# A GQA decode block over a long KV cache: the output weights of the last two heads loaded behind V and multiplied together

## The chip, the cores and the metric

The kernel runs on one core of one Trainium2 chip. The metric is the device time of one execution in microseconds (us). TensorE is written PE, VectorE DVE, ScalarE ACT, GpSimd POOL; SP is the sync engine, which here does nothing but issue loads and stores. All data is float32.

## The reference, cut to what matters

Two tokens (batch B = 2, one position each, width D = 512) pass through a decode block: layer norm, attention with 32 query heads over 8 cached key/value heads of 32768 positions, an output projection, and a gated side branch.

```python
xn = _layernorm(x)                                   # x [2, 1, 512]
q = (xn @ wq).reshape(B, 1, 32, 128)                 # wq [512, 4096]
k, v = k_cache, v_cache                              # [2, 8, 32768, 128], each head used by 4 query heads
p = softmax(einsum("bhqd,bhkd->bhqk", q, k) * 128 ** -0.5)
o = einsum("bhqk,bhkd->bhqd", p, v)
s = o.reshape(B, 1, 4096) @ wo                       # wo [4096, 512]
gate, up = xn @ W_gate, xn @ W_up                    # [512, 1792] each
g = silu((gate * (gate > 0) * up) @ W_down)          # [1792, 512]
return x + s * g
```

Nearly all bytes are the two caches: 2 x 8 x 32768 x 128 x 4 bytes, 268 MB each.

## The kernel before, in words

There are 16 groups, one for each pair of KV head `hk` and batch `b`; group `g` has `b = g % 2` and `hk = g // 2`, so the two batches of a head follow each other. Each group has eight tiles of K and eight of V, 4096 positions or 2 MB each: 128 tiles of each in all, tile `t` in group `t // 8`.

All large loads go through one queue, SP's (`load`, L123), into one ring of eight slots of 2 MB (`SLOTS`). A load is issued when its slot has been given up by whatever was in it eight loads earlier. The output weights of a head (`load_wo`, four query heads, 512 rows of wo, 1 MB) take a slot of the same ring.

The main loop runs over steps `s`. Step `s` transposes K tile `s` on DVE in two halves (`k_transposes`, L287, tile `kts`) and multiplies it with the queries on PE (`scores`, L298); DVE scales the scores into `sc` and keeps the running maximum (L308). The values of a tile come `OFF` = 9 steps later, since a group's softmax needs the maximum over its eight tiles: `maximum` (L314 and on), then `weights` for a tile (exponential on ACT, L338; a permuting matmul `pt` on PE, L342; a transpose `pts` on DVE, L346), then `values` (L355), which accumulates in `o_ps`. After a group's last V tile `sums` gives the reciprocal of the softmax sum, `take_o` (L377) scales `o_ps` into `os`, and `finish_group` brings the result into the layout of the projection: 16 small matmuls into `po` (L386) and two copies into `ot` (L396).

After the second batch of a head, `finish_group` also projects: 16 matmuls of `ot` with that head's weights into `py` (L401). For heads 0 to 6 DVE adds `py` to `yacc` (L410). For head 7 it forms the result: `res = py * gy` and `res += base` (L412, L413), where `gy` is the side branch and `base = yacc * gy + x` was made before (`make_base`, L423, L424). `res` holds the output in four quarters of 128 columns at partitions 0, 32, 64 and 96; four stores of 1 KB, one on POOL's queue, two on SP's and one on ACT's, write them out (L470).

The order of the loads is written out in the lists `ahead`: step `s` issues V tile `s - 6` and K tile `s + 3`, and the output weights of a head stand right behind the last V tile of its second batch. So the weights of head 6 stand in the middle of the stream, between a V tile and the next K tile, and those of head 7 behind everything. Behind the last K tile come eight whole V tiles and the last one, which is loaded in three pieces, of a half and two quarters (`LAST = (2, 1, 1)`); `values` multiplies these pieces one after the other. On each engine the instructions keep an order that is fixed when the program is built; it is close to the program's but not the same: small work such as head 6's projection is placed between the score matmuls of a later step.

Of the kernel before, what the change touches and what calls it, by code (L numbers as in the profile page):

```python
# [8 lines left out]
F32 = mybir.dt.float32  # L9
# [4 lines left out]
P = 128  # L14
# [3 lines left out]
NBLK = NC * NJ  # L18
TK = P * NBLK
LAG = 1  # L20
LAST = (2, 1, 1)
SLOTS = 8
DEPTH = 3
ALIGN = 512
# [3 lines left out]
def kernel(  # L28
# [12 lines left out]
    nc = tc.nc  # L41
    B, HKV, SK, DH = kc.shape
# [4 lines left out]
    NU = SK // TK  # L47
# [10 lines left out]
    const = ctx.enter_context(tc.tile_pool(name="const", bufs=1))  # L58
# [4 lines left out]
    ps_m = ctx.enter_context(tc.tile_pool(name="ps_m", bufs=2, space=PSUM))  # L63
# [19 lines left out]
    n = 1  # L83
# [24 lines left out]

    qt = const.tile([P, B, HKV, 4, Q], F32, name="qt")
    nc.vector.memset(qt, 0.0)  # L110
    ot = const.tile([P, 2, 2, 32], F32, name="ot")
    nc.vector.memset(ot, 0.0)
    yacc = const.tile([P, P], F32, name="yacc")
    nc.vector.memset(yacc, 0.0)
    gy = const.tile([P, P], F32, name="gy")
    base = const.tile([P, P], F32, name="base")
    res = const.tile([P, P], F32, name="res")
# [3 lines left out]
    KT, VT, ST, PT, KTS, NBIAS, LS, MX, WO = {}, {}, {}, {}, {}, {}, {}, {}, {}  # L121
    def load(dst, src):
        nc.sync.dma_start(dst, src)  # L123

    def group(g):
        return g % B, g // B

    def load_tile(dst, src, t, pieces):
        b, hk = group(t // NU)
        lo = (t % NU) * TK  # L130
        rows = src[b, hk, lo : lo + TK, :].rearrange("(p r) d -> p (r d)", p=P)
        flat = dst.rearrange("p c j d -> p (c j d)")
        c = 0
        for n in pieces:
            part = slice(c * NJ * DH, (c + n) * NJ * DH)
            load(flat[:, part], rows[:, part])
            c += n
# [5 lines left out]
    def load_v(t):  # L143
        VT[t] = ring.tile([P, NC, NJ, DH], F32, tag="r", align_bytes=ALIGN, name=f"v_{t}")
        load_tile(VT[t], vc, t, (NC,) if t < NG * NU - 1 else LAST)

    def load_wo(hk):
        WO[hk] = ring.tile([P, 2, 2, D], F32, tag="r", align_bytes=ALIGN, name=f"wo_{hk}")
        r = REP * DH
        load(  # L150
            WO[hk].rearrange("p c i d -> p c (i d)"),
            wo[hk * r : (hk + 1) * r, :].rearrange("(c p i) d -> p c (i d)", c=2, i=2),
        )


    QW = wq.shape[1] // 2
# [191 lines left out]
    def values(t):  # L348
        g, u = divmod(t, NU)
        v, w = VT.pop(t), PT.pop(t)  # L350
        c = 0
        for n in (NC,) if t < NK - 1 else LAST:
            for j in range(NJ):
# [24 lines left out]

    def finish_group(g):
        b, hk = group(g)  # L380
        pr = ps_m.tile([P, 512], F32, tag="m", name=f"po_{g}")
        o2 = OS.pop(g).rearrange("p c (q i) -> p c i q", i=2)
        for i in range(2):
            for r in range(2):
                for c in range(NC):
                    nc.tensor.matmul(  # L386
                        pr[64 * r : 64 * r + 64, i * REP : (i + 1) * REP],
                        o2[:, c, i, :],
                        sel[:, c, :],
                        start=(c == 0),  # L390
                        stop=(c == NC - 1),
                    )
        o3 = pr[:, : 2 * REP].rearrange("p (i c r) -> p c i r", i=2, r=2)
        for r in range(2):
            part = slice(64 * r, 64 * r + 64)
            nc.vector.tensor_copy(ot[part, :, :, b], o3[part, :, :, r])  # L396
        if b == B - 1:
            py = ps_m.tile([P, 512], F32, tag="m", name=f"py_{g}")
            for k in range(4):
                for c in range(4):  # L400
                    nc.tensor.matmul(  # L401
                        py[32 * c : 32 * c + 32, :P],
                        ot[:, k // 2, k % 2, :],
                        WO[hk][:, k // 2, k % 2, c * P : (c + 1) * P],
                        start=(k == 0),
                        stop=(k == 3),
                    )
            WO.pop(hk)
            if hk < HKV - 1:
                nc.vector.tensor_add(yacc, yacc, py[:, :P])  # L410
            else:
                nc.vector.tensor_mul(res, py[:, :P], gy)  # L412
                nc.vector.tensor_add(res, res, base)  # L413

    NK = NG * NU
    OFF = NU + LAG
    extra, ahead = {}, {}

    def at(where, s, f, *a):
        where.setdefault(s, []).append((f, a))  # L420
# [10 lines left out]
        at(ahead, i + 2 - DEPTH, load_gu, "u", i)  # L431
        at(ahead, i + 4 - DEPTH, load_d, i)
    for hk in range(HKV):
        at(ahead, (hk * B + B) * NU - 1 + OFF - DEPTH, load_wo, hk)
    at(extra, 2, mlp_gu, "g")
    at(extra, 4, mlp_gu, "u")
    at(extra, 4, mlp_h)
# [10 lines left out]
    for s in range(NK + OFF):  # L448
        v = s - OFF
        if s < NK:  # L450
            k_transposes(s)
            scores(s)
        if 0 <= v + 1 < NK:
            if (v + 1) % NU == 0:
                maximum((v + 1) // NU)
            weights(v + 1)
        for f, a in extra.get(s, []):
            f(*a)
        if v >= 0:
            if v % NU == NU - 1:  # L460
                sums(v // NU)
            values(v)
            if v % NU == NU - 1:
                take_o(v // NU)
                finish_group(v // NU)
        for f, a in ahead.get(s, []):
            f(*a)

    for c, eng in enumerate((nc.gpsimd, nc.sync, nc.scalar, nc.sync)):
        eng.dma_start(out[:, 0, c * P : (c + 1) * P], res[32 * c : 32 * c + B, :])  # L470


_INS = ["A_x", "A_k_cache", "A_v_cache", "A_wq", "A_wo", "B_W_gate", "B_W_up", "B_W_down"]
# [28 lines left out]
```

## Time and profile before

| | |
|---|---|
| time, median of 3 runs | 1333.25 us (1332.27 to 1333.82) |
| profiled execution | 1335.89 us |
| its span | 1334.0 us |
| granted PE clock, mean over the span | 0.841 |
| PE busy | 881.1 us (66%) |
| DVE busy | 736.5 us (55%) |
| ACT busy | 69.1 us (5%) |
| loads | 564.68 MB on SP's queue, 99.4% of the DMA engines' time |

The profile is of one execution. Its page gives the busy time of each engine, the clock granted to PE and the DMA rate over 40 equal slices of the span, and the costliest groups of instructions with the idle time ahead of them and what ended it. A timeline lists instructions in order of time: start, length, engine, line and operation, output and inputs, how many were merged, and in brackets the idle time before. A row of a stretch lists its start and end, its length, then for PE, PEld (weight loads), DVE, ACT and POOL the busy time with the number of instructions, then the granted clock (1.00 is full), the busy share of the DMA engines and GB/s. One matmul of float32 is two records on PE. A row of a single line gives the shortest, median and longest of its instructions in nanoseconds and when the first and last began; the row on landing gives the time from the issue of a load to its last byte.

### The profile page before, as it was taken

The numbers are of one execution on the slowest core, as the hardware profiler recorded it, in microseconds if no ns is written. First come the engines' busy times: TensorE is split into PE (matmuls) and PEld (weight loads), VectorE is DVE, ScalarE is ACT, GpSimd is POOL, SyncE is SP. The second block draws the span as 40 slices with busy tenths as digits, with TensorE's granted clock in tenths as the row PEclk, the third lists the DMA queues.
The fourth block names the chain that finished last, engine by engine and source line by source line (L and its number), as shares of the span: only waits on it lengthen the run. The fifth ranks groups of instructions, "written<-read, shape, count | busy, mean of one in ns | idle before, by whom it ended". The sixth has DMA issues, their size and how long they took to land.

```text
span 1334.0 us, 17338 instructions
## 1 busy us (share of the span) xinstructions
PE 881.1 (66%) x7560; PEld 345.6 (26%) x7560; DVE 736.5 (55%) x976; ACT 69.1 (5%) x261; POOL 1.3 (0%) x7
## 2 busy tenths in 40 slices
PE   4767566766757666676666757667666766767657
PEld 1333222222213222232222312223222232213213
DVE  5765554555555555564555555465565555556462
ACT  0001010100101001010100101001010100101001
POOL 0000000000000000000000000000000000000000
PEclk9777887988878888788977888888887978878889
DMA  9999999999999999999999999999999999999996
GB/s 397 429 431 429 431 430 430 429 431 431 429 430 431 430 430 430 429 430 432 430 430 422 428 430 431 429 416 429 429 430 430 415 430 429 431 431 414 430 430 283
DMA packets 40907, 565.79 MB, mean 424 GB/s; under 512 B 4462, under 2 KB 4478, under 8 KB 6784
## 3 DMA queue, kind: packets, MB, share of 16 engines
q1 hardware_dynamic: 40776, 564.68, 99.4%
q8 instruction: 60, 0.98, 0.3%
q14 instruction: 15, 0.12, 0.0%
q10 hardware_dynamic: 24, 0.01, 0.0%
q0 software_dynamic: 32, 0.00, 0.0%
HBM read 564.67 MB, written 0.00 MB: 423 GB/s over the span
## 4 chain that ended last, share of the span: by engine, by line
issue 100%; POOLq 0%; POOL 0%
POOLq L497 0%; POOL ident masks.py:199 0%; POOL ident masks.py:197 0%; POOLq masks.py:199 0%; POOLq L484 0%
## 5 line engine op out<-in xcount | busy, mean ns | idle before, releaser
L298 PE MATMUL s<-kts,qt 128*32 128x256 f32 x4096 | 466.7, 522 | 388.9 <-DVE kts L287 373.7
L287 DVE STREAM_TRANSPOSE kts<-k 128x2048 f32<-128x2048 f32 x256 | 572.7, 2275 | 0.0
L355 PE MATMUL o_ps<-v,pts 128*16 128x512 f32 (+2 forms) x2080 | 360.2, 675 | 0.0
L298 PEld LDWEIGHTS s<-kts,qt 128*32 128x32 f32 x4096 | 180.2, 140 | 664.3 <-issue 351.6
L308 DVE TENSOR_SCALAR_CACHE_REDUCE sc<-s 128x256 f32<-128x256 f32 x128 | 54.3, 425 | 375.5 <-PE s L298 375.5
L346 DVE STREAM_TRANSPOSE pts<-pt 128x256 f32<-128x256 f32 x128 | 57.0, 448 | 137.9 <-PE o_ps L355 131.2
L355 PEld LDWEIGHTS o_ps<-v,pts 128*16 128x16 f32 (+2 forms) x2080 | 96.2, 116 | 141.6 <-issue 130.1
L338 ACT ACTIVATE sc<-sc,nb 128x256 f32<-128x256 f32 x128 | 63.2, 494 | 1147.3 <-DVE nb L332 1147.3
L342 PE MATMUL pt<-sc,perm 128*128 128x256 f32 x256 | 85.3, 439 | 33.4 <-DVE pts L346 32.2
L342 PEld LDWEIGHTS pt<-sc,perm 128*128 128x128 f32 x256 | 42.5, 198 | 99.7 <-issue 73.0
L386 PE MATMUL po<-sel,os 128*64 128x4 f32 x512 | 23.4, 204 | 3.9 <-DVE os L377 3.9
L386 PEld LDWEIGHTS po<-sel,os 128*64 128x64 f32 x512 | 22.0, 138 | 10.2 <-DVE os L377 10.2
L338 ACT ACTIVATION_READ_ACCUMULATOR sc<-sc,nb 128x1 f32 x128 | 23.9, 187 | 0.0
L377 DVE TENSOR_SCALAR os<-o_ps,rl 128x512 f32<-128x512 f32 x16 | 12.0, 750 | 17.3 <-PE o_ps L355 17.3
L401 PE MATMUL py<-wo,ot 128*32 128x128 f32 x256 | 19.2, 403 | 0.4 <-DVE ot L396 0.4
L396 DVE COPY ot<-po 64x4 f32<-64x4 f32 x32 | 5.2, 163 | 19.7 <-PE po L386 19.5
L401 PEld LDWEIGHTS py<-wo,ot 128*32 128x32 f32 x256 | 14.1, 153 | 2.5 <-issue 1.5
L192 PE MATMUL pq<-wq,xnt 128*32 128x512 f32 x64 | 10.1, 788 | 1.1 <-DMA wq<-in_A_wq_dram 0.8
L308 DVE DVE_READ_ACCUMULATOR sc<-s 128x1 f32 x128 | 10.7, 83 | 0.0
L180 PE MATMUL px<-ident,boot 32*128 32x32 f32 x4 | 0.9, 288 | 12.8 <-DVE boot L174 12.8
L214 DVE COPY qt<-pqt 32x16 f32<-32x16 f32 x64 | 8.6, 176 | 1.3 <-PE pqt L209 0.9
L332 DVE COPY nb<-pr 128x1 f32<-128x1 f32 x16 | 2.5, 159 | 12.2 <-PE pr L328 12.2
(70 smaller groups left out, 115.3 us busy)
## 6 DMA issues: line engine op xcount, KB each, us to landing
k<-in_A_k_cache_dram SPq DMA_DIRECT2D x128, 2048.0 KB, 18.7
v<-in_A_v_cache_dram SPq DMA_DIRECT2D x127, 2048.0 KB, 17.2
wq<-in_A_wq_dram SPq DMA_DIRECT2D x4, 2048.0 KB, 13.3
wo<-in_A_wo_dram SPq DMA_DIRECT2D x8, 1024.0 KB, 15.5
wg<-in_B_W_gate_dram SPq DMA_DIRECT2D x2, 1792.0 KB
wu<-in_B_W_up_dram SPq DMA_DIRECT2D x2, 1792.0 KB, 33.0
wd<-in_B_W_down_dram SPq DMA_DIRECT2D x2, 1792.0 KB
v<-in_A_v_cache_dram SPq DMA_DIRECT2D x1, 1024.0 KB
```

The source lines that it names most:

```text
L192: nc.tensor.matmul(pq[half][32 * c : 32 * c + 32, :], xnt[:, k, :], wqt[k][:, half, c * 512 : (c + 1) * 512], start=(k == 0), stop=(k == N ...
L214: nc.vector.tensor_copy(qt[part, b, half * 4 : half * 4 + 4, :, kb * REP + h], src[:, :, :, b],)
L287: nc.vector.transpose(KTS[t][:, i * half : (i + 1) * half], src[:, i * half : (i + 1) * half])
L298: nc.tensor.matmul(ps[Q * c : Q * c + Q, :], qt[:, b, hk, e, :], mov[:, e, c], start=(e == 0), stop=(e == 3),)
L308: nc.vector.tensor_scalar(ST[t], ps, SCALE, None, op0=ALU.mult, op1=ALU.max, accum_out=MX[g][:, u : u + 1])
L338: nc.scalar.activation(st, st, AF.Exp, bias=NBIAS[g], scale=1.0, accum_out=LS[g][:, u : u + 1])
L342: nc.tensor.matmul(ps, perm.rearrange("p k c h -> p (k c h)"), st, start=True, stop=True)
L346: nc.vector.transpose(PT[t].rearrange("p j m -> p (j m)"), ps)
L355: nc.tensor.matmul(o_ps[a : a + n * REP, :n, :], w[:, j, c * REP : (c + n) * REP], v[:, c : c + n, j, :], start=(u == 0 and j < 4), stop=( ...
L377: nc.vector.tensor_scalar(OS[g], o_ps, RL.pop(g), None, op0=ALU.mult)
L386: nc.tensor.matmul(pr[64 * r : 64 * r + 64, i * REP : (i + 1) * REP], o2[:, c, i, :], sel[:, c, :], start=(c == 0), stop=(c == NC - 1),)
L401: nc.tensor.matmul(py[32 * c : 32 * c + 32, :P], ot[:, k // 2, k % 2, :], WO[hk][:, k // 2, k % 2, c * P : (c + 1) * P], start=(k == 0), s ...
```

## The change

Four things change.

- The output weights of head 6 are no longer loaded in the middle of the stream but, like head 7's, behind the last V tile; head 7's come after them, in two loads of half a megabyte.
- Head 6's projection is not made when its group ends. After the last group, one product over both heads, 32 matmuls accumulating in one `py`, is multiplied by `gy` and added to `base`. Only heads 0 to 5 go through `yacc`, so `base` can be made one head earlier. As the results of two heads must be kept, `ot` becomes `ots` with two places.
- The last V tile comes in two halves.
- Two stores of 2 KB, one for each batch row, on SP's and on ACT's queue, replace the four.

```diff
-LAST = (2, 1, 1)
+LAST = (2, 2)
...
-    ot = const.tile([P, 2, 2, 32], F32, name="ot")
-    nc.vector.memset(ot, 0.0)
+    ots = const.tile([P, 2, 2, 2, 32], F32, name="ots")
+    nc.vector.memset(ots, 0.0)
...
     def load_wo(hk):
...
-        load(
-            WO[hk].rearrange("p c i d -> p c (i d)"),
-            wo[hk * r : (hk + 1) * r, :].rearrange("(c p i) d -> p c (i d)", c=2, i=2),
-        )
+        dst = WO[hk].rearrange("p c i d -> p c (i d)")
+        rows = wo[hk * r : (hk + 1) * r, :].rearrange("(c p i) d -> p c (i d)", c=2, i=2)
+        if hk < HKV - 1:
+            load(dst, rows)
+        else:
+            for c in range(2):
+                load(dst[:, c], rows[:, c])
...
     def finish_group(g):
         b, hk = group(g)
+        ot = ots[:, hk % 2]
...
-        if b == B - 1:
-            py = ps_m.tile([P, 512], F32, tag="m", name=f"py_{g}")
+        if b == B - 1 and hk < HKV - 2:
+            py = project_o((hk,))
+            nc.vector.tensor_add(yacc, yacc, py[:, :P])
+        elif b == B - 1 and hk == HKV - 1:
+            py = project_o((hk - 1, hk))
+            nc.vector.tensor_mul(res, py[:, :P], gy)
+            nc.vector.tensor_add(res, res, base)
+
+    def project_o(hks):
+        py = ps_m.tile([P, 512], F32, tag="m", name=f"py_{hks[0]}")
+        for hk in hks:
+            w = WO.pop(hk)
             for k in range(4):
                 for c in range(4):
                     nc.tensor.matmul(
                         py[32 * c : 32 * c + 32, :P],
-                        ot[:, k // 2, k % 2, :],
-                        WO[hk][:, k // 2, k % 2, c * P : (c + 1) * P],
-                        start=(k == 0),
-                        stop=(k == 3),
+                        ots[:, hk % 2, k // 2, k % 2, :],
+                        w[:, k // 2, k % 2, c * P : (c + 1) * P],
+                        start=(hk == hks[0] and k == 0),
+                        stop=(hk == hks[-1] and k == 3),
                     )
-            WO.pop(hk)
-            if hk < HKV - 1:
-                nc.vector.tensor_add(yacc, yacc, py[:, :P])
-            else:
-                nc.vector.tensor_mul(res, py[:, :P], gy)
-                nc.vector.tensor_add(res, res, base)
+        return py
...
     for hk in range(HKV):
-        at(ahead, (hk * B + B) * NU - 1 + OFF - DEPTH, load_wo, hk)
+        end = hk if hk < HKV - 2 else HKV - 1
+        at(ahead, (end * B + B) * NU - 1 + OFF - DEPTH, load_wo, hk)
...
-    for c, eng in enumerate((nc.gpsimd, nc.sync, nc.scalar, nc.sync)):
-        eng.dma_start(out[:, 0, c * P : (c + 1) * P], res[32 * c : 32 * c + B, :])
+    rows = res.rearrange("(c q) n -> q c n", q=32)
+    for b, eng in enumerate((nc.sync, nc.scalar)):
+        eng.dma_start(out[b, 0, :].rearrange("(c n) -> c n", c=4), rows[b])
```

In the built program the 16 matmuls with head 6's weights stand on PE directly behind the last group's `po` matmuls and wait for their load alone; those with head 7's weights follow and wait for the two copies into `ots` and for their loads. On SP the first of the two loads of head 7's weights waits for the slot of the V tile eight loads ahead of it, the second tile of the last group.

## The prediction

> **What bounds the kernel now.** I read the page first, then the waits, the landings of single loads, and at last the timeline with the granted clock in short stretches. The chain that ended last is put down to "issue" for 100% of the span and tells nothing here.
>
> ```profile
> span 1334.0 us, 17338 instructions
> GB/s 397 429 431 429 431 430 430 429 431 431 429 430 431 430 430 430 429 430 432 430 430 422 428 430 431 429 416 429 429 430 430 415 430 429 431 431 414 430 430 283
> L287 DVE STREAM_TRANSPOSE kts<-k 128x2048 f32<-128x2048 f32 x256 | 572.7, 2275 | 0.0
> SPq L123 <- PE o_ps L355: 568.6, 120, 10.4
> ```
>
> The DMA engines move 430 GB/s nearly throughout, so the kernel looks bound by its loads. Yet the K transposes (L287), first reader of every K tile, never wait for one (idle 0.0); the load queue instead waits for the engines to free slots. So DVE and PE pace the loop, taking turns (the rows below show it), the loads keep up, and a load that comes earlier changes nothing by itself. The same holds near the end:
>
> ```profile
> L123 SPq DMA_DIRECT2D v<-in_A_v_cache_dram x7: 327/328/328, 1272.7 to 1298.2; - x7
> DMA to landing us min/median/max: 15.7/15.7/16.2
> 1311.38 1.91 PE L355 MATMUL o_ps<-v,pts 128*16 128x512 f32 x16
> L123 SPq DMA_DIRECT2D wo<-in_A_wo_dram x1: 378/378/378, 1310.2 to 1310.2; - x1
> DMA to landing us min/median/max: 15.5/15.5/15.5
> ...
> DMA to landing us min/median/max: 17.6/18.2/18.7
> ```
>
> The second of those seven V tiles, issued at 1278.0, lands at 1293.7 and is multiplied at 1311.38. The last wo, issued at 1310.2, lands at 1325.7. The last row is of the last V tile's small pieces, the longest there.
>
> What decides the pace is the granted clock. First the stretches in which a group *without* a projection works on its first K tile, then one *with* it (head 6's, the one that goes):
>
> ```profile
> 1149.72:1153.14 3.42, 2.09 (x20) 0.80 (x20) 1.74 (x2) 0.00 (x0) 0.00 (x0) 0.50 1.05 450
> 1153.14:1156.55 3.41, 3.41 (x26) 1.06 (x22) 0.43 (x2) 0.00 (x0) 0.00 (x0) 0.50 0.95 408
> 1156.55:1159.96 3.41, 1.72 (x12) 0.40 (x4) 2.31 (x2) 0.00 (x0) 0.00 (x0) 1.00 1.03 442
> ...
> 1224.82:1228.23 3.41, 3.01 (x39) 2.33 (x38) 1.91 (x7) 2.93 (x12) 0.00 (x0) 1.00 0.97 413
> 1228.23:1231.64 3.41, 2.59 (x16) 1.42 (x19) 3.41 (x3) 0.00 (x0) 0.00 (x0) 0.50 1.06 452
> 1231.64:1235.06 3.42, 3.42 (x51) 2.63 (x49) 1.93 (x5) 0.00 (x0) 0.00 (x0) 0.50 0.98 422
> 1235.06:1238.47 3.41, 2.76 (x31) 1.10 (x22) 1.35 (x4) 0.00 (x0) 0.00 (x0) 1.00 0.99 413
> 1241.88:1245.30 3.42, 2.85 (x28) 1.35 (x32) 0.51 (x1) 0.00 (x0) 0.00 (x0) 0.50 1.02 436
> 1245.30:1248.71 3.41, 2.76 (x22) 0.71 (x14) 1.62 (x4) 0.00 (x0) 0.00 (x0) 1.00 0.99 423
> ```
>
> The columns are the stretch, its length, busy PE, PEld, DVE, ACT, POOL, then the clock. Each stretch has one clock, 1.00 or 0.50. After a half-clock stretch in which PE was busy 2.09 or 2.59 us the next is again at 0.50; after 2.85, 3.41 or 3.42 us it is at 1.00.
>
> The Trainium skill ("TensorE: Matmul & The Clock Gate", Part 1) describes a free-running window of 3413 ns, a half clock after an idle window and a full one after a busy window; the rows agree, and show besides that "busy" means more than 2.59 of 3.41 us.
>
> **The change, part by part.**
>
> *Head 6's projection leaves the middle.* Sixteen matmuls and the addition to yacc go from the first step of the last group.
>
> ```profile
> 1140.29 0.16 DVE L314 TENSOR_REDUCE m<-mx 128x1 f32<-128x8 f32 x1
> 1155.15 0.42 DVE L308 TENSOR_SCALAR_CACHE_REDUCE sc<-s 128x256 f32<-128x256 f32 x1 [3.69 <-PE s L298]
> 1157.65 0.45 DVE L346 STREAM_TRANSPOSE pts<-pt 128x256 f32<-128x256 f32 x1 [2.07 <-PE o_ps L355]
> 1221.52 0.16 DVE L314 TENSOR_REDUCE m<-mx 128x1 f32<-128x8 f32 x1
> 1228.19 4.46 DVE L287 STREAM_TRANSPOSE kts<-k 128x2048 f32<-128x2048 f32 x2
> 1231.43 1.74 PE L401 MATMUL py<-wo,ot 128*32 128x128 f32 x26
> 1235.84 0.43 DVE L308 TENSOR_SCALAR_CACHE_REDUCE sc<-s 128x256 f32<-128x256 f32 x1 [1.45 <-PE s L298]
> 1237.56 0.45 DVE L346 STREAM_TRANSPOSE pts<-pt 128x256 f32<-128x256 f32 x1 [1.28 <-PE o_ps L355]
> 1293.37 0.42 DVE L308 TENSOR_SCALAR_CACHE_REDUCE sc<-s 128x256 f32<-128x256 f32 x1 [2.02 <-PE s L298]
> 1300.71 0.16 DVE L314 TENSOR_REDUCE m<-mx 128x1 f32<-128x8 f32 x1
> ```
>
> The projection sits at 1231.43, while PE would wait for the second half of the transposes (they end at 1232.65), so taking it out frees no time that counts. But it is what keeps PE busy for all of 1231.64 to 1235.06. Without it the scores alone fill that stretch from about 1232.7, 2.35 us, below the 2.59 us after which the clock stayed at half. So I expect 1235.06 to 1238.47 at 0.50 too. Then sc takes what it took in the group without a projection, 1155.15 less 1151.41 (transposes from 1146.95, as long), 3.74 us: 1232.65 + 3.74 = 1236.39. There pts came 2.50 us after sc, the half clock ending 1.40 us after sc; here it ends 2.08 us after, 0.68 us more, which costs 0.34 us: pts at 1239.23 instead of 1237.56, **+1.7 us**.
>
> What follows is paced by the same stretches. From one maximum (L314) to the next the group without projection takes 1221.52 - 1140.29 = 81.23 us, the one with it 1300.71 - 1221.52 = 79.19 us, a difference of 2.04 us. I take **+2.0 us** for the loop, near the +1.7 of its first step. The work then meets the stretches later than before, and one more can fall to half clock:
>
> ```profile
> 1304.44 1.46 PE L386 MATMUL po<-sel,os 128*64 128x4 f32 x32 [0.19 <-DVE os L377]
> 1308.20 1.91 PE L355 MATMUL o_ps<-v,pts 128*16 128x512 f32 x16
> ```
>
> Counted on in steps of 3.413 us from 1224.82, the stretches near the end have edges at 1306.74 and 1310.15. Two microseconds later, po runs from 1306.5 and the values product from 1310.2, so this stretch holds only po and the small transposing products, like 1224.82 to 1228.23, whose 3.01 busy microseconds were followed by 0.50. The values product then takes 3.5 instead of 1.91 us; a score product at half clock costs as much (sc waited 3.69 there, 2.02 at 1293.37). I take one such, **+1.6 us**; ends: none, 0, and two, +3.3.
>
> *The end.*
>
> ```profile
> 1324.60 1.63 PEld L355 LDWEIGHTS o_ps<-v,pts 128*8 128x8 f32 x44 [0.32 <-issue]
> 1327.40 1.46 PE L386 MATMUL po<-sel,os 128*64 128x4 f32 x32 [0.87 <-DVE os L377]
> 1328.89 0.34 DVE L396 COPY ot<-po 64x4 f32<-64x4 f32 x2 [1.55 <-PE po L386]
> 1329.29 0.81 PEld L401 LDWEIGHTS py<-wo,ot 128*32 128x32 f32 x32 [0.52 <-DVE ot L396]
> 1329.29 1.08 PE L401 MATMUL py<-wo,ot 128*32 128x128 f32 x32 [0.43 <-DVE ot L396]
> 1331.08 0.65 SPq L470 DMA_DIRECT2D out_dram<-res  x2
> 1331.35 0.65 POOL L470 DMA_DIRECT2D out_dram<-res  x1 [1330.04 <-DVE res L413]
> ```
>
> Head 6's product now stands behind po and ahead of head 7's. It needs nothing from the copies, so it starts when po ends (1328.86) and issues for 0.81 us; head 7's starts at 1329.67 instead of 1329.29: **+0.4 us**. Were it to wait for the copies, it would cost its whole 1.08. The last V tile in two pieces: 32 quarter-width records become 16 half-width ones. By columns the work is equal; the 44 small records went at 37 ns each, hardly above the matmuls' own pace. I take **-0.1** (ends -0.3 and 0). Stores: POOL's issue ends at 1332.00, SP's second at 1331.73, and a single SP issue, half of the pair's 0.65, at 1331.4. If a store lands equally long after its issue, 0.3 to 0.6 us go; four rows for a store instead of two could give 0.3 back. I take **-0.4** (ends -0.6 and 0).
>
> *What costs nothing.* Head 6's load leaves SP's queue ahead of the last group's K and V, which come earlier to engines that don't wait for them. At the end it stands behind V, and head 7's must wait for the slot of the V tile multiplied at 1311.38, free at 1313.3; at 15.5 us to landing this is 1328.8, ahead of 1329.67. That cover is only 0.9 us on the old timetable, some 4 us on mine. The doubled ots is cleared in the idle time before the first loads; the base computation moves one head earlier, beside a wait of sc for PE:
>
> ```profile
> 7.70 0.67 DVE L167 TENSOR_REDUCE st<-boot 32x1 f32<-32x512 f32 x1 [2.85 <-DMA boot<-in_A_x_dram]
> 1075.41 0.42 DVE L308 TENSOR_SCALAR_CACHE_REDUCE sc<-s 128x256 f32<-128x256 f32 x1 [2.11 <-PE s L298]
> ```
>
> **Sum.** +2.0 + 1.6 + 0.4 - 0.1 - 0.4 = +3.5 us: from the profiled execution's 1335.89 us (span 1334.0) to 1339.4. The plain runs have a median of 1333.25 (1332.27 to 1333.82), 2.64 lower; I put the same difference on it: 1336.7 us. No change that can be told is 0.2% here, 2.7 us.
>
> **The rivals.** *A, the forecast:* the clock stays at half one stretch longer. Chance 0.70, of which 0.20 for no further half stretch (+1.9 us, within 0.2%), 0.38 for one (+3.5) and 0.12 for two (+5.2).
>
> *B, the clock comes back as before.* If 2.35 us of unbroken score products are enough, the loop keeps its old times, and only the end counts: -0.1 us, 1333.1. Against it speak 2.09 and 2.59 us followed by 0.50; for it, that part of the 2.59 were transposing products, which may count less, as after 1224.82. It decides if the clock over 1235.06 to 1238.47 is 1.00. Chance 0.17. The Trainium skill's page on the clock gate, Part 1, read by its letter (only an idle window throttles) gives this case; here no row shows 2.35 us of scores alone.
>
> *C, faster:* without the projection the steps meet the stretches so that two fewer are at half clock. Each is worth at most 1.7 us (half of 3.41), so -0.1 - 3.4 = -3.5: 1329.8 us. For it speaks that steps with sc waiting 2.02 exist; against it, that less PE work makes the clock rise later and not sooner in every row above. Chance 0.10.
>
> *D, the last load is late:* if head 7's wo needs the 18.7 us of the slowest small piece from its slot at 1313.3 while the loop keeps its old pace, it lands at 1332.0, 2.3 us after its matmuls could start: 1333.1 + 2.3 = 1335.4 us. It decides from 16.4 us to landing on; 15.5 was measured. Chance 0.03.
>
> **How the numbers follow.** Slower by over 0.2%: 0.38 + 0.12 = 0.50. Within: 0.20 + 0.17 + 0.03 = 0.40. Faster: 0.10. The range goes from 1331.9 (B with the end's best terms, 0.4 - 0.3 - 0.6 = -0.5, and 0.8, half the spread of the runs) to 1338.9 (A with two half stretches, 1338.4, and half a microsecond towards the end's worst). It leaves out C and the extremes. A's own range is 1335.1 to 1338.9.
>
> **What would show it.** Right: no projection near 1231 us, the clock at 0.50 up to some 6 us past the end of that step's transposes, 81 us or more between the last two maxima. The final product in 64 records of some 1.9 us in all, its first half beside the copies, and no POOL store. Wrong: about 79.2 us between those maxima (B), fewer (C), or PE's last product waiting for a wo load (D).

## The result, and the profile after

The changed kernel takes 1336.59 us (median of 20 runs, 1330.48 to 1339.99), the kernel before, run beside it, 1333.67 us (20 runs, 1332.27 to 1336.53): a ratio of 1.0020, 95% interval 1.0013 to 1.0028, or 2.9 us more. The profiled execution took 1335.82 us with a span of 1334.0 us, the same span as before. This execution reached the steady part of its loop 3.35 us sooner than the one profiled before (1218.17 against 1221.52 us at the last maximum but one), and lost as much in the last group and the end. I take the head start for chance: the first maximum comes at 103.3 to 110.7 us in the thirteen profiles, and the medians differ by 2.9 us all the same. So intervals are compared here, and not points of time. One of the twenty runs, of 1330.48 us, had a mean granted clock of 0.852 where the others had 0.835 to 0.842; e2 comes back to it.

The timeline of the kernel after, DVE's part (start, length, engine, line and operation, names, and in brackets the idle time before it and what ended it); the maximum is line L317 here, the K transposes are L290, `sc` is L311 and `pts` L349:

```profile
1136.95 0.16 DVE L317 TENSOR_REDUCE m<-mx 128x1 f32<-128x8 f32 x1
1218.17 0.16 DVE L317 TENSOR_REDUCE m<-mx 128x1 f32<-128x8 f32 x1
1224.83 4.46 DVE L290 STREAM_TRANSPOSE kts<-k 128x2048 f32<-128x2048 f32 x2
1233.02 0.42 DVE L311 TENSOR_SCALAR_CACHE_REDUCE sc<-s 128x256 f32<-128x256 f32 x1 [3.69 <-PE s L301]
1235.88 0.45 DVE L349 STREAM_TRANSPOSE pts<-pt 128x256 f32<-128x256 f32 x1 [2.42 <-PE o_ps L358]
1300.30 0.16 DVE L317 TENSOR_REDUCE m<-mx 128x1 f32<-128x8 f32 x1
```

The interval ahead of the last one is 81.22 us, as before. The last one is 1300.30 - 1218.17 = 82.13 us, where it was 79.19. That is +2.94 us, as much as the medians differ by (2.92). The granted clock in the same place, in stretches of 3.41 us (columns as in the prediction: the stretch, its length, busy PE, PEld, DVE, ACT, POOL, then the clock):

```profile
1224.89:1228.30 3.41, 2.58 (x8) 0.84 (x6) 3.41 (x3) 0.00 (x0) 0.00 (x0) 0.50 1.00 428
1228.30:1231.72 3.42, 2.39 (x25) 1.15 (x28) 1.03 (x2) 0.00 (x0) 0.00 (x0) 0.50 1.02 436
1231.72:1235.13 3.41, 3.41 (x22) 0.82 (x16) 0.43 (x2) 0.00 (x0) 0.00 (x0) 0.50 0.99 418
1235.13:1238.54 3.41, 1.36 (x8) 0.30 (x2) 2.66 (x3) 0.00 (x0) 0.00 (x0) 1.00 1.04 447
1238.54:1241.96 3.42, 2.26 (x16) 0.81 (x20) 2.17 (x1) 0.00 (x0) 0.00 (x0) 0.50 0.97 417
1241.96:1245.37 3.41, 3.41 (x30) 1.26 (x26) 0.43 (x2) 0.00 (x0) 0.00 (x0) 0.50 1.01 432
```

The second of these is the stretch that held the projection and was busy for all of its 3.42 us. Now the scores alone keep PE busy for 2.39 us, the next stretch stays at 0.50, and the values product, which DVE's `pts` waits for, runs in it at half speed. The stretch after that holds only 1.36 us of work at full clock, and so the second step's scores, too, start at half clock; its first half-clock stretch is busy 2.26 us and again does not bring the clock back.

The end, from the timelines of before and of after:

```profile
1326.59 0.75 DVE L377 TENSOR_SCALAR os<-o_ps,rl 128x512 f32<-128x512 f32 x1 [4.72 <-PE o_ps L355]
...
1330.44 0.29 DVE L412 TENSOR_TENSOR res<-py,gy 128x128 f32<-128x128 f32 x1 [1.20 <-PE py L401]
1330.76 0.29 DVE L413 TENSOR_TENSOR res<-res,base 128x128 f32<-128x128 f32 x1
```

```profile
1326.17 0.75 DVE L380 TENSOR_SCALAR os<-o_ps,rl 128x512 f32<-128x512 f32 x1 [4.71 <-PE o_ps L358]
1328.37 1.95 PE L415 MATMUL py<-wo,ots 128*32 128x128 f32 x64
1328.48 0.34 DVE L400 COPY ots<-po 64x4 f32<-64x4 f32 x2 [1.55 <-PE po L390]
1330.39 0.29 DVE L406 TENSOR_TENSOR res<-py,gy 128x128 f32<-128x128 f32 x1 [1.57 <-PE py L415]
1330.72 0.29 DVE L407 TENSOR_TENSOR res<-res,base 128x128 f32<-128x128 f32 x1
1331.04 0.65 SPq L481 DMA_DIRECT2D out_dram<-res  x1
```

Counted from the last maximum, `os` comes after 1326.59 - 1300.71 = 25.88 us before and 25.87 after, so the last V tile in two halves changes nothing. `res` starts after 29.73 and 30.09 us: the longer product costs 0.36. From the end of the last DVE operation to the end of the span it is 1334.0 - 1331.05 = 2.95 and 1334.0 - 1331.01 = 2.99 us: two stores or four, it is the same.

### The profile page after: what moved, and what is told of

Same layout as the page of the kernel before. It is cut to its first block, busy times and chain, and to the rows that moved or that the text cites. A ratio compares the mean times of both kernels' runs of the same rounds, so it can differ in the third digit from the quotient of the medians.

```text
span 1334.0 us, 17305 instructions
## 1 busy us (share of the span) xinstructions
PE 880.8 (66%) x7544; PEld 341.9 (26%) x7544; DVE 736.4 (55%) x975; ACT 69.1 (5%) x261; POOL 0.7 (0%) x6
## 4 chain that ended last, share of the span: by engine, by line
PE 49%; DVE 46%; issue 3%; DMA 2%; ACT 0%; DVEq 0%
DVE kts L290 41%; PE s L301 25%; PE o_ps L358 18%; DVE pts L349 2%; PE po L390 2%; DMA wq<-in_A_wq_dram 2%; PE pt L345 1%; DVE sc L311 1%; PE py L415 1%; DVE os L380 1%; PE ps_g L239 0%; PE pr L331 0%; DVE qt L217 0%; PE pr L319 0%; PE pqt L212 0%
## 5 line engine op out<-in xcount | busy, mean ns | idle before, releaser
L290 DVE STREAM_TRANSPOSE kts<-k 128x2048 f32<-128x2048 f32 x256 | 572.8, 2275 | 0.0
L358 PE MATMUL o_ps<-v,pts 128*16 128x512 f32 (+1 forms) x2064 | 363.9, 686 | 0.0
L311 DVE TENSOR_SCALAR_CACHE_REDUCE sc<-s 128x256 f32<-128x256 f32 x128 | 54.3, 425 | 372.8 <-PE s L301 372.7
L349 DVE STREAM_TRANSPOSE pts<-pt 128x256 f32<-128x256 f32 x128 | 57.0, 448 | 140.8 <-PE o_ps L358 134.1
L358 PEld LDWEIGHTS o_ps<-v,pts 128*16 128x16 f32 (+1 forms) x2064 | 96.2, 117 | 144.6 <-issue 133.5
L415 PE MATMUL py<-wo,ots 128*32 128x128 f32 x256 | 17.5, 384 | 0.0
L400 DVE COPY ots<-po 64x4 f32<-64x4 f32 x32 | 5.2, 163 | 19.7 <-PE po L390 19.5
L415 PEld LDWEIGHTS py<-wo,ots 128*32 128x32 f32 x256 | 13.0, 146 | 1.8 <-issue 1.3
L311 DVE DVE_READ_ACCUMULATOR sc<-s 128x1 f32 x128 | 10.7, 83 | 0.0
L335 DVE COPY nb<-pr 128x1 f32<-128x1 f32 x16 | 2.5, 158 | 12.2 <-PE pr L331 12.2
## 6 DMA issues: line engine op xcount, KB each, us to landing
wq<-in_A_wq_dram SPq DMA_DIRECT2D x4, 2048.0 KB, 13.4
```

The costliest lines, as they stand in the source:

```text
L290: nc.vector.transpose(KTS[t][:, i * half : (i + 1) * half], src[:, i * half : (i + 1) * half])
L311: nc.vector.tensor_scalar(ST[t], ps, SCALE, None, op0=ALU.mult, op1=ALU.max, accum_out=MX[g][:, u : u + 1])
L349: nc.vector.transpose(PT[t].rearrange("p j m -> p (j m)"), ps)
L358: nc.tensor.matmul(o_ps[a : a + n * REP, :n, :], w[:, j, c * REP : (c + n) * REP], v[:, c : c + n, j, :], start=(u == 0 and j < 4), stop=( ...
L415: nc.tensor.matmul(py[32 * c : 32 * c + 32, :P], ots[:, hk % 2, k // 2, k % 2, :], w[:, k // 2, k % 2, c * P : (c + 1) * P], start=(hk == ...
```

## The experiments

Each is compared with runs of the kernel before made beside it on the same chip, whose medians were 1333.46 us (e1 to e4), 1332.90 (e5 to e8) and 1333.20 (e9 to e11). Theory A is the prediction's: the clock stays at half one stretch longer where the projection is missing.

**e1: head 6 back in the middle, the other edits kept.**

```diff
-        if b == B - 1 and hk < HKV - 2:
+        if b == B - 1 and hk < HKV - 1:
...
-            py = project_o((hk - 1, hk))
+            py = project_o((hk,))
...
-        end = hk if hk < HKV - 2 else HKV - 1
-        at(ahead, (end * B + B) * NU - 1 + OFF - DEPTH, load_wo, hk)
+        at(ahead, (hk * B + B) * NU - 1 + OFF - DEPTH, load_wo, hk)
```

> Undoes the move alone: head 6's weights are loaded and multiplied in the middle again, while the last V tile in two halves, the two loads of head 7's weights and the two stores stay as in the changed kernel. Theory A (head 6's product keeps PE busy in a stretch of 3.41 us, and so brings the clock back one stretch sooner): 79.2 us between the last two maxima, as in the kernel before; from the last maximum to the end 33.3 us; ratio to the kernel before 1.000, within 0.1%. Rival T (the end of the kernel pays: stores, pieces of V, weights behind V): the stores and the V pieces alone would show here as up to 1.002, with 79.2 us between the maxima and over 33.6 us behind the last one.

Measured: 1334.06 us, ratio 1.0005 (0.9997 to 1.0014). The last interval:

```profile
1220.34 0.16 DVE L317 TENSOR_REDUCE m<-mx 128x1 f32<-128x8 f32 x1
1299.52 0.16 DVE L317 TENSOR_REDUCE m<-mx 128x1 f32<-128x8 f32 x1
```

It is 79.18 us again. The V tile in halves, the two stores and the divided load of head 7's weights together move the time by nothing that can be told.

**e2: only the move.** The last V tile, head 7's load and the stores are those of before.

```diff
-LAST = (2, 2)
+LAST = (2, 1, 1)
...
-        if hk < HKV - 1:
-            load(dst, rows)
-        else:
-            for c in range(2):
-                load(dst[:, c], rows[:, c])
+        load(dst, rows)
...
-    for b, eng in enumerate((nc.sync, nc.scalar)):
-        eng.dma_start(out[b, 0, :].rearrange("(c n) -> c n", c=4), rows[b])
+    for c, eng in enumerate((nc.gpsimd, nc.sync, nc.scalar, nc.sync)):
+        eng.dma_start(out[:, 0, c * P : (c + 1) * P], res[32 * c : 32 * c + B, :])
```

> The move alone: both heads' weights behind V and multiplied together, but V in three pieces, head 7's weights in one load and four stores as in the kernel before. Theory A: about 82.1 us between the last two maxima, 33.7 us behind the last one, ratio to the kernel before 1.002. Rival T: if V's pieces, the split load or the stores are what costs, 1.000 to 1.001.

Measured: 1336.27 us, ratio 1.0012 (0.9997 to 1.0027). The interval includes no difference; it is wide because 4 of its 12 runs took 1331.0 to 1331.8 us and the others 1334.4 to 1339.8. In the profiled run, of 1335.35 us, the last interval is 82.12 us:

```profile
1217.75 0.16 DVE L313 TENSOR_REDUCE m<-mx 128x1 f32<-128x8 f32 x1
1299.87 0.16 DVE L313 TENSOR_REDUCE m<-mx 128x1 f32<-128x8 f32 x1
```

So in this execution the move alone makes the long interval. In the four shorter runs the mean granted clock was 0.849 to 0.856, in the others 0.838 to 0.842, so they met the clock otherwise, as did the one short run of after; no profile shows where.

**e3: the same work twice.** The kernel after, but head 6's weights are also loaded where they were before and multiplied there, and that product is thrown away.

```diff
+        elif b == B - 1 and hk == HKV - 2:
+            project_o((hk,))
...
+        if hk == HKV - 2:
+            at(ahead, (hk * B + B) * NU - 1 + OFF - DEPTH, load_wo, hk)
```

> The changed kernel, in which head 6's weights are loaded and multiplied in the middle as well, and that product is thrown away: 1 MB more to load, 16 matmuls more, no addition on DVE. Theory A: the useless product brings the clock back, so 79.2 us between the last two maxima, 33.7 us behind the last one, ratio to the kernel before 1.0003 (+0.4 us for the longer last product), some 2.5 us less than the changed kernel though it does more. Rival T: as the changed kernel or worse, ratio 1.002 to 1.004 (1 MB at 430 GB/s is 2.4 us). Rival D (the late loads of the weights hold up the last product): worse than the changed kernel by the 2.4 us that everything behind lands later.

Measured: 1334.78 us, ratio 1.0009 (1.0000 to 1.0017), and a last interval of 79.19 us:

```profile
1217.62 0.16 DVE L317 TENSOR_REDUCE m<-mx 128x1 f32<-128x8 f32 x1
1296.81 0.16 DVE L317 TENSOR_REDUCE m<-mx 128x1 f32<-128x8 f32 x1
```

With 1 MB more to load and 16 matmuls more, the last interval is 2.94 us shorter than after's. Work that nobody needs pays for itself. Only part of it reaches the end (1334.78 against 1336.59 us): the profile shows PE waiting 0.90 us for the last half of V, ahead of which 1 MB more was loaded, and `py` taking 2.96 us instead of 1.95.

**e4: no projection in the middle at all.** This kernel leaves out the projections of heads 0 to 6, matmuls and additions; their weights are still loaded.

```diff
-        if b == B - 1:
+        if b == B - 1 and hk == HKV - 1:
```

> The kernel before without the projections of heads 0 to 6, matmuls and additions (their weights are still loaded): it leaves out work that the output needs. Theory A: every group is then without a projection, seven of them take 81 to 82 us instead of 79.2, so +14 to +20 us, ratio 1.010 to 1.015. Rival W (PE or DVE work in the loop costs time, and less of it never hurts): ratio 1.000 or below, down to 0.990 (1.4 us for each product).

Measured: 1332.69 us, ratio 0.9995 (0.9987 to 1.0004). This expectation was far off. Without any projection the loop does not become slower by 2 to 3 us for each, but settles on another pattern:

```profile
1057.58 0.16 DVE L314 TENSOR_REDUCE m<-mx 128x1 f32<-128x8 f32 x1
1136.07 0.16 DVE L314 TENSOR_REDUCE m<-mx 128x1 f32<-128x8 f32 x1
1214.55 0.16 DVE L314 TENSOR_REDUCE m<-mx 128x1 f32<-128x8 f32 x1
1296.10 0.16 DVE L314 TENSOR_REDUCE m<-mx 128x1 f32<-128x8 f32 x1
```

Intervals of 78.49 and 78.48 us, with one of about 82 among them every few groups (three, besides one of 81.23 near the start and the last of 81.55). A group without a projection is therefore not long as such. The stretches of a short group, then of a long one:

```profile
1060.64:1064.05 3.41, 3.01 (x39) 2.17 (x38) 1.91 (x6) 3.17 (x14) 0.00 (x0) 1.00 0.97 413
1064.05:1067.47 3.42, 1.72 (x8) 0.73 (x8) 3.42 (x3) 0.00 (x0) 0.00 (x0) 1.00 1.04 441
1217.66:1221.07 3.41, 3.01 (x39) 2.17 (x38) 1.91 (x6) 3.12 (x14) 0.00 (x0) 1.00 0.95 408
1221.07:1224.48 3.41, 2.77 (x8) 1.24 (x8) 3.41 (x3) 0.00 (x0) 0.00 (x0) 0.50 1.06 447
1224.48:1227.90 3.42, 2.38 (x26) 1.02 (x28) 1.24 (x2) 0.00 (x0) 0.00 (x0) 0.50 1.01 431
```

The first stretch of each holds the same work, 3.01 us of it, but begins 3.06 us behind the maximum in the short group and 3.11 in the long one; after that the clock stays up in the one and falls in the other. This holds beyond e4. In the traces of all kernels but e5 and e6, that stretch is busy 3.01 or 3.02 us in 85 groups: in the 17 in which it begins 3.04 to 3.10 us behind the maximum the next is at full clock, in the 68 in which it begins 3.11 to 3.30 us behind it (3.30 in the last group of after) at half. (One of 2.98 us, in the second group of e7, fell at 3.08.) So the phase, the place of the stretches against the maximum, decides, and a group's time follows from it. What at the edge of the stretch makes the difference is open.

78.49 us are 23.0 stretches of 3.413 us and 82.0 are 24.0; in the kernel before two groups together, 160.42 us, are 47.0. The loop locks to the stretches of the clock, and an edit shifts it from one whole number to another.

**e5 and e6: PE kept busy in every step,** in the kernel before (e5) and in the kernel after (e6). In each K step two useless matmuls run between the first and the second half of the transposes.

```diff
         ps = ps_s.tile([P, 256], F32, tag="s", name=f"s_{t}")
+        pd = ps_m.tile([P, 512], F32, tag="m", name=f"pd_{t}")
+        for i in range(2):
+            nc.tensor.matmul(
+                pd[:, :384], ident, KTS[t][:, i * 512 : i * 512 + 384], start=(i == 0), stop=(i == 1)
+            )
```

> The kernel before, with two matmuls added in each of the 128 K steps that multiply the first half of the transposed tile (384 columns each) into a tile nobody reads, so that PE is busy while it waits for the second half of the transposes. Theory A (PE that is not busy enough in a 3.41 us stretch falls to half clock, and the half clocks pace the loop): the mean granted clock goes from 0.86 to above 0.95, the intervals between maxima (79.19 and 81.23 before) go to 79.0 or less, at the lowest what the loads allow (17 transfers of 2 MB in a group of 33.6 MB and half a wo at 430 GB/s, 79.2 us on average), and the run to about 1329 us (1326 to 1332), though PE does more work. Rival T (the work itself paces the loop, the clock only follows): two more matmuls of 0.5 to 1 us each in 128 steps make the run longer, 1340 us or more.

> The kernel after, with the same two matmuls in each K step. Theory A: the move costs what it does only by the half clock behind the removed projection. With the clock kept up there is no such stretch, the last interval between maxima is no longer than the others of this run, and this kernel stands within -2.5 to +0.5 us of the kernel before with the same additions (the last V tile lands some 2.4 us sooner, the end costs the 0.4 us measured). Rival (the move costs by itself, by its slot, its queue or its longer end): it is 2.5 to 3.5 us slower than the other one with additions, as after was against before.

Measured: e5 1332.03 us, ratio 0.9989 (0.9980 to 0.9999); e6 1331.43 us, ratio 0.9982 (0.9973 to 0.9991). More work in 128 steps makes both shorter, against rival T; but the mean clock rose only to 0.88, not above 0.95, and e5 stands at the upper bound of what was expected (1332). The list of waits of e5 says why:

```profile
DVE kts L287 <- DMA k<-in_A_k_cache_dram: 60.0, 37, 3.9
```

The K transposes now wait 60.0 us in all for their loads, 37 times; before they never did. The loads were only just hidden, and they take over as soon as the engines get faster. With the loads as the limit the move costs nothing: e6 is 0.6 us below e5, within the bounds expected of A. As the loads and not the clock pace both, this doesn't tell whether the clock is the cause; the next experiments do.

**e7 and e8: how much work brings the clock back.** As e3, but with 8 (e7) and 4 (e8) of the 16 matmuls in the middle.

```diff
-            project_o((hk,))
+            project_o((hk,), 2)
...
-    def project_o(hks):
+    def project_o(hks, nk=4):
...
-            for k in range(4):
+            for k in range(nk):
...
-                        stop=(hk == hks[-1] and k == 3),
+                        stop=(hk == hks[-1] and k == nk - 1),
```

(The diff is e7's; e8 passes 1 instead of 2.)

> The kernel after, with head 6's weights also loaded ahead of the last group and 8 of the 16 matmuls of its product also done in the middle (thrown away). Theory A, with a threshold between 2.60 and 2.73 busy microseconds in a stretch: at half clock the 8 matmuls keep PE busy some 0.6 us of the stretch that was busy 2.38 without them, 3.0 us, so the clock comes back as with all 16: last interval 79.2 us, run 1334.8 us, as with 16. Rival, graded (each matmul in the middle buys its share): half of the 2.94 us, last interval 80.7, run 1335.7.

> The same with 4 of the 16 matmuls in the middle. Theory A: some 0.2 to 0.3 us more in the stretch that was busy 2.38 us, 2.6 to 2.7, at the threshold; I expect the clock to stay at half, as without any: last interval 82.1 us, run 1336.6 us; it can fall to 79.2 where the execution meets the stretches at another phase, but not between. Rival, graded: a quarter of the 2.94 us back, last interval 81.4.

Measured: e7 1334.50 us, ratio 1.0012 (1.0003 to 1.0021); e8 1335.03, ratio 1.0010 (1.0001 to 1.0019). Both have a last interval of 79.19 us (maxima at 1219.50 and 1298.70 in e7, at 1215.78 and 1294.97 in e8): e7 as expected, e8 not. The stretch that held the projection and the next one, in e3, e7 and e8:

```profile
1227.74:1231.15 3.41, 3.41 (x51) 2.62 (x49) 1.06 (x2) 0.00 (x0) 0.00 (x0) 0.50 0.99 423
1231.15:1234.57 3.42, 2.77 (x32) 1.12 (x23) 1.34 (x4) 0.00 (x0) 0.00 (x0) 1.00 1.04 417
1229.63:1233.05 3.42, 3.24 (x37) 1.55 (x33) 1.03 (x2) 0.00 (x0) 0.00 (x0) 0.50 0.98 422
1233.05:1236.46 3.41, 2.76 (x26) 0.82 (x18) 1.38 (x4) 0.00 (x0) 0.00 (x0) 1.00 1.04 437
1225.90:1229.32 3.42, 2.81 (x29) 1.18 (x28) 1.05 (x2) 0.00 (x0) 0.00 (x0) 0.50 0.96 412
1229.32:1232.73 3.41, 2.76 (x26) 0.82 (x18) 1.38 (x4) 0.00 (x0) 0.00 (x0) 1.00 1.02 432
```

This is the same stretch in all, 10.1 us behind the maximum, so that the phase is not what differs. It is busy 2.39 us in after, 2.81 with 4 matmuls, 3.24 with 8 and 3.41 with 16 (e3). After 2.39 the next is at 0.50, after the three others at 1.00. So it is a step and not a slope, between the 2.59 us of the prediction's row and 2.81. The traces of all kernels but e5 and e6 agree: of their 1174 half-clock stretches from 120 us on, the 216 busy up to 2.61 us are all followed by half clock, the 939 busy 2.81 us or more all by full, and the 19 between go both ways. In e8 I had the size of the dose wrong (0.2 to 0.3 us instead of 0.42), not the threshold. That e8 is no faster as a whole, though its last maximum came at 1294.97 us, has the cause that e3 showed: PE waits 2.2 us for the last V tiles, and as the clock falls meanwhile, `po` and `py` take 2.03 and 3.64 us instead of 1.46 and 1.95.

**e9 and e10: matmuls that load nothing.** The kernel after, with 16 (e9) or 2 (e10) matmuls with the identity as their moving operand in the place where the projection was.

```diff
+        elif b == B - 1 and hk == HKV - 2:
+            pd = ps_m.tile([P, 512], F32, tag="m", name=f"pd_{g}")
+            for k in range(4):
+                for c in range(4):
+                    nc.tensor.matmul(
+                        pd[32 * c : 32 * c + 32, :P],
+                        ots[:, hk % 2, k // 2, k % 2, :],
+                        ident,
+                        start=(k == 0),
+                        stop=(k == 3),
+                    )
```

> The kernel after, with sixteen matmuls of the removed projection's shape in the place where it was, but with the identity as their moving operand, so that nothing more is loaded; their product is thrown away. Theory A (busy microseconds in one 3.41 us stretch are all that counts): that stretch is filled again, the last interval between maxima is 79.2 us (82.13 without them), and the run stands at the kernel before plus the 0.4 us of the longer end, 1333 to 1334 us, 2.5 us below after. Rival L (what was gained by the earlier variants came from loading head 6's weights early, out of the queue at the end): the last interval stays at 82.1 and the run at 1336.6, since the loads here are those of after.

> The same with two such matmuls instead of sixteen. In the stretch that counts PE was busy 2.38 us without any, 2.81 with four and 3.23 with eight, the first followed by half clock, the others by full. Two should give 2.5 to 2.6, below the 2.60 after which the clock has stayed at half wherever score products ended the stretch: last interval 82.1 us, run 1336.6. Were the threshold nearer to 2.4 than to 2.7, it would be 79.2 and 1333.7.

Measured: e9 1332.86 us, ratio 0.9996 (0.9988 to 1.0005); e10 1335.43 us, ratio 1.0020 (1.0011 to 1.0029). The last intervals are 78.72 us in e9 and 82.13 in e10:

```profile
1214.58 0.16 DVE L317 TENSOR_REDUCE m<-mx 128x1 f32<-128x8 f32 x1
1293.30 0.16 DVE L317 TENSOR_REDUCE m<-mx 128x1 f32<-128x8 f32 x1
```

```profile
1217.60 0.16 DVE L317 TENSOR_REDUCE m<-mx 128x1 f32<-128x8 f32 x1
1299.73 0.16 DVE L317 TENSOR_REDUCE m<-mx 128x1 f32<-128x8 f32 x1
```

All loads are those of after, so rival L falls: sixteen matmuls that compute nothing give back what the move cost. They do it in a slightly other way than foreseen. They ran 6.2 us behind the maximum, at 1220.76 us, where the projection before came 9.9 us behind it, and the stretches from 1217.89 to 1231.54 stayed at 1.00 throughout. e10 is no clean measure of a dose of two for the same reason: they ran ahead of the stretch that counts, which was busy 2.37 us, as without them. They did keep the stretch before it at 1.00 (1224.32 to 1227.73, at 0.50 in after), and that alone left the interval at 82.13.

**e11: the same sixteen behind every group without a projection.**

```diff
-        elif b == B - 1 and hk == HKV - 2:
+        elif b == 0 or hk == HKV - 2:
```

(against e9)

> The kernel after, with the sixteen thrown-away matmuls behind every group that has no projection (nine of them) and not behind the one alone. Theory A: the other intervals of 81.23 us are long for the same reason as the last one of after, a first step at half clock one stretch longer; all intervals go to about 79.2 us, where the loads (33.6 MB and on average half a wo at 430 GB/s, 79.2 us) begin to limit. The loop is up to 14 us shorter, then the last V tiles are waited for; the run ends when the loads allow it, 1330 us (1328 to 1332.5). Rival T (the alternation of 79.2 and 81.2 comes from something else of the two halves of a head, such as their loads): intervals stay at 79.2 and 81.2, the run at 1334.

Measured: 1330.73 us, ratio 0.9982 (0.9973 to 0.9991), with e6 the fastest, faster than both kernels. Three of four intervals are 78.4 to 79.2 us, and the fourth is 81.4, which A did not foresee; the last maximum comes at 1286.92 us instead of 1300.71 in the kernel before. The loop has become nearly 14 us shorter and the run 2.5. The timeline shows where the rest went:

```profile
1286.92 0.16 DVE L317 TENSOR_REDUCE m<-mx 128x1 f32<-128x8 f32 x1
...
1314.83 1.91 PE L358 MATMUL o_ps<-v,pts 128*16 128x512 f32 x16 [3.06 <-DMA v<-in_A_v_cache_dram]
1317.27 1.05 PE L358 MATMUL o_ps<-v,pts 128*8 128x256 f32 x16 [0.52 <-DMA v<-in_A_v_cache_dram]
1319.61 1.05 PE L358 MATMUL o_ps<-v,pts 128*8 128x256 f32 x16 [1.30 <-DMA v<-in_A_v_cache_dram]
```

The last V tiles set the end. With e6 at 1331.43 us this is what the loads leave: some 1331 us, 2.5 us below the kernel before.

## Why the prediction was right

*The clock stays at half one stretch longer (+1.7 us in the first step): right in mechanism and size.* PE was busy 2.39 us where 2.35 was worked out, the next stretch was at 0.50, `sc` came 3.73 us after the end of the transposes (3.74 predicted) and `pts` 2.86 us after `sc` (2.84 worked out). From the maximum to `pts` it is 17.71 us, where it was 16.04: +1.67. e3, e7 and e8 put matmuls back into that stretch, at the same phase, and the clock and the interval came back with them; e9 did it without a load. So the cause is shown and not only argued. The Trainium skill ("TensorE: Matmul & The Clock Gate", HAM oscillation) gives as the rule that PE must not idle for more than about 3.4 us; here 1.03 idle microseconds in a stretch at half clock (2.39 of 3.42 busy) kept it there, and 2.05 in one at full clock (1.36 of 3.41 busy) were followed by half, so the traces ask for more than the rule does. Nor do the prediction's rows agree, as it says, with a fall only after an idle stretch: the one at 1224.82 was busy 3.01 us and was followed by half clock.

*The loop as a whole (+2.0) and one more half-clock stretch (+1.6): the kind was right, the place and the size were not.* One more did come, but in the second step (1238.54 to 1245.37) and not near the end, and there it brought the loop's part from 1.67 to 2.94 us, 1.3 instead of 1.6. The group did not become one of 81.23 us, as I had it from the groups without a projection, but one of 82.13: in those a stretch begins 2.60 us behind the maximum (1142.89, two stretches ahead of 1149.72), in this one 3.30, so their first steps are not alike. Near the end the stretch that I expected at half clock stayed at full:

```profile
1303.40:1306.81 3.41, 3.01 (x39) 2.17 (x38) 1.90 (x6) 3.13 (x14) 0.00 (x0) 1.00 0.99 423
1306.81:1310.22 3.41, 3.21 (x22) 1.18 (x22) 0.73 (x4) 0.00 (x0) 0.00 (x0) 1.00 1.02 430
```

The stretch with `po` and the transposing products was busy 3.01 us and was followed by full clock, where the row that I argued from (also 3.01) was followed by half. So a number of busy microseconds at full clock does not tell by itself. The two differ in phase: this one begins 3.10 us behind its maximum, that one 3.30, on the two sides of what e4's rows show. Of the sum, 2.0 + 1.6 = 3.6 became 2.94.

*The longer product, +0.4:* 0.36 measured. It started when `po` ended and beside the copies, as forecast.

*The last V tile in halves, -0.1:* 0.0, its better end being the wrong one.

*The stores, -0.4:* 0.0, the end of its range at which four rows in a store give back what fewer stores save. One store of four rows took 0.65 us to issue on SP, as long as the pair before. This term failed; e1 bears it out: all small edits together come to +0.6 us, and the interval of that ratio includes no difference.

The measured terms give 2.94 + 0.36 = +3.3 us against +3.5 forecast and +2.9 between the medians, 1336.59 us against 1336.7. That it came so near is partly luck: the loop's terms were 0.7 too high and the end's 0.5 too low, and the second stretch at half clock came in a step where the prediction had none.

*The rivals.* B (the clock comes back as before) and C (two stretches fewer) are excluded by the rows of after; C has a grain of truth, though, since e4 and the first half of e8 show that groups of 78.5 us exist, with projections and without, in another pattern of the loop. The argument against it, that less PE work makes the clock rise later, fails in e4, whose mean clock is 0.855 against 0.841 before. D did not come. The view of the load line for the end of after has the loads of the last weights, their first and last start, and the time to landing:

```profile
L123 SPq DMA_DIRECT2D wo<-in_A_wo_dram x3: 328/379/424, 1309.8 to 1313.3; - x3
...
DMA to landing us min/median/max: 10.3/11.1/12.2
```

The last of them was there by 1313.3 + 12.2 = 1325.5 us, and the product that needs it began at 1328.37, with head 6's half. The cover was 3 us and, with that half, some 4, as worked out.

What the prediction left out is the other side of "the loads keep up": they do so by about 2.5 us over the whole run. Of the variants that gave the loop its time back, e3, e8, e9 and e11 waited for the last V tiles; e7, whose last maximum came latest of them (1298.70 us), did not.

## What to carry to other kernels

Where the clock of TensorE changes in fixed stretches, matmuls in a gap are not free to remove: look up how busy the stretch is that they stand in, and what the clock does in the next. Before counting on a faster loop, look at how far the next limit is: here the loads were 0.2% behind the engines. And if a loop's intervals are whole numbers of stretches, the price of an edit can't be read from one group and multiplied by their number.

## What was not expected of the hardware

- The loop locks to the clock's stretches so well that intervals repeat within 0.03 us over whole runs (79.19 and 81.23 us), and there are at least three patterns (79.2 with 81.2; 78.5 with 82.0; 78.4 to 79.2 with 81.4). Which of them a run falls into is not decided by the edit alone: e8, the same as after up to the last group but for one load, ran its first groups in the second, and e9, with the loads of after, its first in the third.
- Thrown-away matmuls make this kernel faster: the kernel with 16 of them takes 2.6 us less than the one with two (e9 against e10), and 144 of them put the last maximum 13.4 us sooner than in after (e11, 1286.92 against 1300.30 us).
- Where the loads set the end, the DMA engines are only partly busy there. In e11 it is a share of 0.57, for 8.5 us, while V tiles are still waited for, though all loads had been issued by 1301.1 us (columns as above, the last two being the DMA share and GB/s; the second line is the packets of 1305 to 1311.12 us):

```profile
1313.51:1322.05 8.54, 4.52 (x60) 1.64 (x61) 0.75 (x1) 0.00 (x0) 0.00 (x0) 1.00 0.57 236
DMA packets 319, 2.56 MB, mean 418 GB/s; under 512 B 28, under 2 KB 28, under 8 KB 160
```

  236 GB/s there, 430 in the loop. The Trainium skill ("DMA: Bandwidth & Descriptors", Two DMAs through the same engine are not ordered) says that nothing orders transfers across the sixteen engines; the trace agrees. V comes in pieces of 16 and 8 KB and the last weights in pieces of 4 KB, and 160 - 28 = 132 of these were started between 1305 and 1311.12 us, while the V tiles, which stand ahead of the weights in the queue, were waited for until 1319.61. So weights were moved while PE waited for V; which engine moved what the trace does not say. It is worth up to 8.54 x 0.43 = 3.7 us, an estimate from these rows.
